# Attention decode over a long cache: scores and P·V on four 32-column TensorE tiles, with K^T and V as the moving operand

## Chip, cores, metric

One NeuronCore of one Trainium2 chip. The metric is the device time of one execution in microseconds, where smaller is better. Kernels are compared only within the same rounds. "Span" is the time from the first to the last instruction in a profile; in these runs the device time is about 1.8 us more than the span.

## The reference

A decode step for a single token (batch 1, query length 1, width 512). Attention has 32 query heads and 8 key/value heads of 128, over a cache of 32768 positions. Beside it runs a small gated feed-forward part, and a scalar gate mixes the two. All inputs are bfloat16. Cut to what matters:

```python
q = (x @ wq)                                   # 32 heads of 128
scores = einsum("bhqd,bhkd->bhqk", q, k) * Dh ** -0.5
p = softmax(scores)                            # over 32768 positions
a = einsum("bhqk,bhkd->bhqd", p, v) @ wo       # wo: 4096 x 512
b = (silu(x @ w_gate) * (x @ w_up)) @ w_down
g = sigmoid((x * gate_w).sum())
return g * a + (1 - g) * b
```

The K and V caches are 8 heads x 32768 x 128 x 2 bytes x 2 = 134 MB. With the weights, 148.1 MB have to be read, each byte once, with little arithmetic per byte.

## The kernel before

The loads form one stream into a ring of five slots of 4 MB. The stream's unit is a *half*: one half of the positions of one K or V head, 16384 x 128. Order: Wq, K halves of head 0 with the feed-forward weights between, then K of head g alternating with V of head g-1, then the last head's two V halves, and Wo at the very end. A slot is loaded again as soon as its former content is used.

```python
stream = [("wq",), ("K", 0, 0), ("F1",), ("K", 0, 1), ("F2",)]
for g in range(1, G):
    for hf in range(2):
        stream += [("K", g, hf), ("V", g - 1, hf)]
stream += [("V", G - 1, 0), ("V", G - 1, 1), ("wo",)]
...
# sync engine: one load per entry, once the slot's former content is released
if i >= NSLOT:
    sp.wait_ge(*released[stream[i - NSLOT]])
```

TensorE transposes K, 64 transposes per half. VectorE copies each group of four out of PSUM, the memory in which TensorE's results lie (`ktT`). The scores take K^T as the *stationary* operand: 128 weight loads per half, each followed by a matmul of only 8 columns. P·V, the exponentials times V, takes the exponentials as stationary operand (16 columns) and V as moving operand (512 columns): 32 matmuls per half, one after another.

```python
def emit_scores(j):
    ...
    for t in range(0, TPF, 2):
        for e in range(2):
            pe.matmul(ps_sc[f % NSC][:, col : col + 2 * HPG],
                      kt[:, e, :],            # stationary: K^T, 128 columns
                      qz[:, g, e, :],         # moving: q, 8 columns
                      start=(e == 0), stop=(e == 1))

def emit_pv(g, hf, src, r0, n):
    ...
    for r in range(r0, r0 + n, TPV):
        pe.matmul(ps_pv[0 : TPV * HPG, :],                       # 16 x 512
                  ET[:, g % NEG, k : k + TPV, :]...,             # stationary: 16 columns
                  src[:, r : r + TPV, :]...,                     # moving: V, 512 columns
                  start=(k == 0), stop=(k == NT - TPV))
    ...
def emit_o(g):      # fold the block diagonal of ps_pv (copied to pv_sb) into the head outputs
    ...
# (cut) after the last P·V: normalise, reorder heads, 128 Wo matmuls of one column, output
```

Of the kernel before, what the change touches and what calls it, by code (L numbers as in the profile page):

```python
# [13 lines left out]
def bass_gated_mix__gqa_block_cached__swiglu_ffn__decode_kernel(  # L14
# [18 lines left out]
    HPG = H // G  # L33
# [19 lines left out]
    TPV = 4  # L53
    NKT = 8
    NST = 3
    NSC = 3
    NEG = 3
    LAG = 3
    SCALE = float(DH) ** -0.5
    V_LAST = (64, 32, 16, 16)  # L60
    WO_CUT = (16, 8, 4, 4)
    assert sum(V_LAST) == RH and sum(WO_CUT) == WOJ
# [9 lines left out]
    with ExitStack() as es:  # L72
# [7 lines left out]
        sem_ld = [S_(f"s_ld{i}") for i in range(len(stream) - 2)]  # L80
        sem_ldv = [S_(f"s_ldv{i}") for i in range(len(V_LAST))]
# [38 lines left out]
        sem_osel = S_("s_osel")  # L120
        sem_pvc = S_("s_pvc")
# [13 lines left out]
        ET = T("ET", [128, NEG, NT, HPG], BF16)  # L135
# [22 lines left out]
        qz = T("qz", [128, G, 2, 2 * HPG], BF16)  # L158
# [3 lines left out]
        pmaxf = T("pmaxf", [128, NH, HPG], FP32)  # L162
        pmax = T("pmax", [128, G, HPG], FP32)
        gmax = T("gmax", [128, G, HPG], FP32)
        nbias = T("nbias", [128, G, HPG], FP32)
        esum = T("esum", [128, G, 2, HPG], FP32)
        esum2 = T("esum2", [128, G, HPG], FP32)
        rS = T("rS", [128, H], FP32)
        oidx = T("oidx", [128, TPV * HPG], FP32)
        osel = T("osel", [128, TPV, HPG], FP32)  # L170
        pv_sb = T("pv_sb", [TPV * HPG, TPV * DH], FP32)
# [11 lines left out]
        ps_sc = [ps[:, NST + i, :] for i in range(NSC)]  # L183
        ps_pv = ps[:, 6, :]
# [35 lines left out]
        with nc.Block("main") as block:  # L220

            @block.gpsimd
            def _(pool):
                npool = [0]

                def chain(ins):
# [42 lines left out]
                    oidx[:, :],  # L269
                    pattern=[[HPG, TPV], [1, HPG]],  # L270
                    base=0,
                    channel_multiplier=0,
                    allow_small_or_imprecise_dtypes=True,
                ).then_inc(sem_iota, 1)
                pool.iota(
# [6 lines left out]
                for g in range(G):  # L282
                    pool.wait_ge(sem_pmax, 3 * (g + 1))
                    pool.partition_all_reduce(  # L284
                        gmax[:, g, :], pmax[:, g, :], 128, ReduceOp.max
                    ).then_inc(sem_gmax, 1)

            @block.sync
            def _(sp):
                for i, e in enumerate(stream):  # L290
# [25 lines left out]
                    else:  # L316
# [5 lines left out]
                        if e == ("V", G - 1, 1):  # L322
                            r0 = 0
                            for c, n in enumerate(V_LAST):
                                sp.dma_start(
                                    dst[:, r0 : r0 + n, :], src[:, r0 : r0 + n, :]
                                ).then_inc(sem_ldv[c], 16)
                                r0 += n
                        else:
                            sp.dma_start(dst, src).then_inc(sem_ld[i], 16)  # L330
# [7 lines left out]
            def _(pe):  # L338
# [84 lines left out]
                def emit_scores(j):  # L423
                    f, q = j // FPH, j % FPH
                    g = f // 2
                    if j == 0:
                        pe.wait_ge(sem_qz, 4)
                    if q == 0 and f >= NSC:
                        pe.wait_ge(sem_exp, HPG * (f - NSC + 1))
                    pe.wait_ge(sem_cp, j + 1)  # L430
                    for t in range(0, TPF, 2):
                        col = (q * TPF + t) * HPG
                        kt = ktT[:, j % NKT, t * 128 : (t + 2) * 128].rearrange(
                            "p (k e) -> p e k", e=2
                        )
                        for e in range(2):
                            ins = pe.matmul(  # L437
                                ps_sc[f % NSC][:, col : col + 2 * HPG],
                                kt[:, e, :],
                                qz[:, g, e, :],  # L440
                                start=(e == 0),
                                stop=(e == 1),
                            )
                    ins.then_inc(sem_sc, 1)

                def emit_pv(g, hf, src, r0, n):
                    if r0 == 0 and hf == 0 and g > 0:
                        pe.wait_ge(sem_pvc, g)
                    for r in range(r0, r0 + n, TPV):
                        k = hf * RH + r  # L450
                        ins = pe.matmul(  # L451
                            ps_pv[0 : TPV * HPG, :],
                            ET[:, g % NEG, k : k + TPV, :].rearrange("p r h -> p (r h)"),
                            src[:, r : r + TPV, :].rearrange("p r d -> p (r d)"),
                            start=(k == 0),
                            stop=(k == NT - TPV),
                        )
                    if r0 + n == RH:
                        ins.then_inc(sem_pv, 1)

                def emit_o(g):
# [3 lines left out]
                    for r in range(TPV):  # L465
                        ins = pe.matmul(  # L466
                            ps_m[:, M_OT + g * HPG : M_OT + (g + 1) * HPG],
                            pv_sb[:, r * DH : (r + 1) * DH],
                            osel[0 : TPV * HPG, r, :],
                            start=(r == 0),  # L470
                            stop=(r == TPV - 1),
                        )
# [7 lines left out]
                for e in stream[:-1]:  # L480
                    if e[0] == "K":
                        pe.wait_ge(load_sem(e), 16)
                        for q in range(FPH):
                            emit_fill(filled, kv_slot(e), q)
                            filled += 1
                            if q >= LAG:
                                emit_scores(scored)
                                scored += 1
                            if e[2] == 0 and e[1] >= 2 and q == LAG:
                                emit_o(e[1] - 2)  # L490
                        continue
                    if e[0] != "V":
                        while scored < filled:
                            emit_scores(scored)
                            scored += 1
# [3 lines left out]
                    src = kv_slot(e)  # L499
                    pe.wait_ge(sem_exp, 2 * HPG * g + HPG * (hf + 1))  # L500
                    if e == ("V", G - 1, 1):
                        pe.wait_ge(sem_esum2, 1)
# [3 lines left out]
                            esum2[:, :, :].rearrange("p g h -> p (g h)"),  # L506
# [3 lines left out]
                        emit_o(G - 2)  # L510
                        r0 = 0
                        for c, n in enumerate(V_LAST):
                            pe.wait_ge(sem_ldv[c], 16)
                            emit_pv(g, hf, src, r0, n)
                            r0 += n
                        continue
                    pe.wait_ge(load_sem(e), 16)
                    r0 = 0
                    while scored < filled:
                        emit_pv(g, hf, src, r0, TPF)  # L520
                        r0 += TPF
                        emit_scores(scored)
                        scored += 1
                    emit_pv(g, hf, src, r0, RH - r0)
# [28 lines left out]
            def _(act):  # L553
# [10 lines left out]
                for g in range(G):  # L564
                    act.wait_ge(sem_gmax, g + 1)
                    act.activation(  # L566
                        nbias[:, g, :], gmax[:, g, :], ACT.Copy, scale=-SCALE
                    ).then_inc(sem_nbias, 1)
                    act.wait_ge(sem_nbias, g + 1)
                    if g >= NEG:  # L570
                        act.wait_ge(sem_pv, 2 * (g - NEG + 1))
                    for hf in range(2):
                        f = 2 * g + hf
                        sc = ps_sc[f % NSC].rearrange("p (t h) -> p h t", h=HPG)
                        for h in range(HPG):
                            act.activation(  # L576
                                ET[:, g % NEG, hf * RH : (hf + 1) * RH, h],
                                sc[:, h, :],
                                ACT.Exp,
                                bias=nbias[:, g, h : h + 1],  # L580
                                scale=SCALE,
                                accum_out=esum[:, g, hf, h : h + 1],
                            ).then_inc(sem_exp, 1)

            @block.vector
            def _(dve):
# [6 lines left out]

                dve.wait_ge(sem_pe_x, 1)
# [10 lines left out]
                dve.wait_ge(sem_iota, 4)  # L605
                for i, thr in enumerate((32.0, 64.0, 96.0)):
# [14 lines left out]
                dve.tensor_copy(pmat[:, :], pmat_f[:, :]).then_inc(sem_pm, 1)  # L621
                dve.tensor_scalar(
                    osel[:, :, :].rearrange("p r h -> p (r h)"),
                    oidx[:, :],
                    kf[:, 0:1],
                    None,
                    op0=ALU.is_equal,
                ).then_inc(sem_osel, 1)
# [9 lines left out]
                for e in range(2):  # L638
# [3 lines left out]
                    for b in range(2):  # L642
                        dve.tensor_copy(
                            qz[b * 64 : (b + 1) * 64, :, e, b * HPG : (b + 1) * HPG],
# [24 lines left out]
                def emit_pmax(f):  # L669
                    dve.wait_ge(sem_sc, FPH * (f + 1))  # L670
                    sc = ps_sc[f % NSC].rearrange("p (t h) -> p h t", h=HPG)
                    dve.tensor_reduce(pmaxf[:, f, :], sc, AX.X, ALU.max).then_inc(sem_pmax, 1)  # L672
                    if f % 2 == 1:
                        g = f // 2
                        dve.wait_ge(sem_pmax, 3 * g + 2)
# [82 lines left out]
```

## Time and profile before

| | before |
|---|---|
| median of 3 runs | 359.77 us (359.49 to 359.95) |
| profiled span, mean granted TensorE clock | 357.9 us, 0.967 |
| loads | 148.1 MB; 4 MB alone take 9.8 us at 429 GB/s |
| TensorE busy | 92% |

First the head of the profile's page: busy time of each engine, share of the span, instructions.

```profile
span 357.9 us, 9051 instructions
## 1 busy us (share of the span) xinstructions
PE 327.6 (92%) x4088; PEld 244.8 (68%) x4088; DVE 191.1 (53%) x321; ACT 28.5 (8%) x140; POOL 5.1 (1%) x23
```

TensorE looks like the bound. The next view, busy time of every engine in one stretch of the middle (columns: stretch, its length, busy times, granted TensorE clock, share of the 16 DMA engines, GB/s), says that it is not alone:

```profile
core 0: us, PE busy (x) PEld busy (x) DVE busy (x) ACT busy (x) POOL busy (x), PEclk, DMA share, GB/s
100.00:300.00 200.00, 194.66 (x2321) 142.23 (x2321) 116.76 (x184) 16.00 (x85) 1.86 (x5) 0.99 1.00 429
```

TensorE is busy 194.7 of 200 us, but the DMA engines are busy all of it, at 429 GB/s. The two are level.

The costliest TensorE groups (busy us, mean ns of one | idle before it, and what ended that): transposes of K, P·V, scores.

```profile
L418 PE MATMUL ps<-ident_f,ring 128*128 128x128 f32 x1024 | 161.8, 290 | 9.8 <-DMA ring<-in_A_k_cache_dram 9.8
L451 PE MATMUL ps<-ring,ET 128*16 128x512 bf16 x512 | 120.2, 379 | 0.9 <-DVE pv_sb L684 0.9
...
L437 PE MATMUL ps<-qz,ktT 128*128 128x8 bf16 x2048 | 88.4, 167 | 0.4 <-DVE ktT L690 0.4
```

The two groups that the change is about take 120.2 and 88.4 us. What TensorE waited for, in the list of waits (us in total, times, longest):

```profile
PE ps L418 <- DMA ring<-in_A_k_cache_dram: 9.8, 8, 6.0
```

Only 9.8 us in the whole execution. The end of the span, TensorE alone, in order of time:

```profile
333.45 7.07 PE L451 MATMUL ps<-ring,ET 128*16 128x512 bf16 x32 [0.86 <-DVE pv_sb L684]
...
341.77 7.07 PE L451 MATMUL ps<-ring,ET 128*16 128x512 bf16 x32
349.67 1.05 PE L466 MATMUL ps<-osel,pv_sb 16*128 16x4 f32 x8 [0.82 <-DVE pv_sb L684]
...
351.72 3.57 PE L538 MATMUL ps<-O,ring 128*128 128x1 bf16 x128 [0.28 <-DVE O L716]
```

The last two V halves follow each other without a gap of the load's making, 7.07 us each; then the fold, the Wo matmuls, and the output. The same stretch by what the loads did (columns as above):

```profile
342.00:344.00 2.00, 2.00 (x11) 0.87 (x10) 0.00 (x0) 0.00 (x0) 0.00 (x0) 1.00 1.03 432
...
346.00:348.00 2.00, 2.00 (x11) 0.81 (x9) 0.00 (x0) 0.00 (x0) 0.00 (x0) 1.00 0.64 268
...
350.00:352.00 2.00, 1.18 (x18) 1.00 (x18) 0.60 (x3) 0.00 (x0) 0.00 (x0) 0.86 0.50 203
352.00:354.00 2.00, 2.00 (x81) 2.00 (x79) 0.00 (x0) 0.00 (x0) 0.00 (x0) 0.50 0.02 8
```

The loads fade from 346 us on and are over soon after 352, yet TensorE's last Wo matmul ends at 351.72 + 3.57 = 355.29. At the end TensorE is late.

### The profile page before, as it was taken

Reading aid. Unit: us, or ns where it says so; the run is one execution under the profiler, and the core shown is the slowest. Engines: PE = TensorE matmul, PEld = TensorE weight load, DVE = VectorE, ACT = ScalarE, POOL = GpSimd, SP = SyncE. Lnnn points to the kernel's source line nnn. Section 1 sums busy time; section 2 is a strip of 40 time slices with the busy share of each in tenths; the row PEclk is TensorE's granted clock in tenths of the full one; section 3 lists DMA queues with packets and bytes.
Section 4 is the critical chain, followed back from the end, with each engine's and each line's share of the span. In section 5 each row is a group of like instructions: output and inputs, shape, how many; then the busy total and the mean of one; then the engine's idle time right before and its main releaser. Section 6 shows DMA issues by size and latency. Waiting matters only on the chain.

```text
span 357.9 us, 9051 instructions
## 1 busy us (share of the span) xinstructions
PE 327.6 (92%) x4088; PEld 244.8 (68%) x4088; DVE 191.1 (53%) x321; ACT 28.5 (8%) x140; POOL 5.1 (1%) x23
## 2 busy tenths in 40 slices
PE   0439999999999998999999999999999999999995
PEld 0439999858594957777584939686685949585345
DVE  0229197839292936657391918465472919384001
ACT  1000005000300030000300030001100030003000
POOL 0100000000000000000000000000000000000000
PEclk9999588999999999999999999999989999999996
DMA  8999999999999999999999999999999999999981
GB/s 344 417 405 452 416 431 430 434 419 430 441 416 437 430 430 430 423 436 425 426 435 423 438 423 428 438 430 419 439 420 427 441 416 443 427 423 421 412 365 75
DMA packets 6242, 148.69 MB, mean 415 GB/s; under 512 B 698, under 2 KB 700, under 8 KB 1212
## 3 DMA queue, kind: packets, MB, share of 16 engines
q1 hardware_dynamic: 6200, 148.12, 96.9%
q8 instruction: 32, 0.52, 0.6%
q14 instruction: 6, 0.05, 0.0%
q10 hardware_dynamic: 4, 0.00, 0.0%
HBM read 148.11 MB, written 0.00 MB: 414 GB/s over the span
## 4 chain that ended last, share of the span: by engine, by line
PE 56%; DMA 40%; DVE 2%; issue 1%; SPq 0%; DVEq 0%
DMA ring<-in_A_k_cache_dram 40%; PE ps L418 23%; PE ps L451 20%; PE ps L437 8%; PE ps L387 2%; PE ps L466 1%; PE ps L538 1%; DVE pv_sb L684 1%; DVE ktT L690 1%; PE ps L401 0%; SPq L294 0%; PE ps L503 0%; PE ps L548 0%; DVE row L729 0%; DVE res L720 0%
## 5 line engine op out<-in xcount | busy, mean ns | idle before, releaser
L690 DVE COPY ktT<-ps 128x1024 bf16<-128x1024 bf16 x256 | 168.5, 688 | 96.3 <-PE ps L418 96.0
L418 PE MATMUL ps<-ident_f,ring 128*128 128x128 f32 x1024 | 161.8, 290 | 9.8 <-DMA ring<-in_A_k_cache_dram 9.8
L418 PEld LDWEIGHTS ps<-ident_f,ring 128*128 128x128 f32 x1024 | 113.6, 145 | 18.0 <-DMA ring<-in_A_k_cache_dram 14.7
L451 PE MATMUL ps<-ring,ET 128*16 128x512 bf16 x512 | 120.2, 379 | 0.9 <-DVE pv_sb L684 0.9
L437 PEld LDWEIGHTS ps<-qz,ktT 128*128 128x128 bf16 x2048 | 85.6, 97 | 21.3 <-issue 18.1
L437 PE MATMUL ps<-qz,ktT 128*128 128x8 bf16 x2048 | 88.4, 167 | 0.4 <-DVE ktT L690 0.4
L451 PEld LDWEIGHTS ps<-ring,ET 128*16 128x16 bf16 x512 | 41.3, 89 | 52.4 <-issue 1.3
L672 DVE TENSOR_REDUCE pmaxf<-ps 128x4 f32<-128x512 f32 x16 | 11.1, 692 | 28.1 <-PE ps L437 28.1
L576 ACT ACTIVATE ET<-ps,nbias 128x128 bf16<-128x128 f32 x64 | 23.9, 556 | 0.2
L566 ACT ACTIVATE nbias<-gmax 128x4 f32<-128x4 f32 x8 | 1.6, 205 | 260.8 <-POOL gmax L284 260.8
L576 ACT ACTIVATION_READ_ACCUMULATOR ET<-ps,nbias 128x1 f32 x64 | 18.2, 284 | 0.0
L684 DVE COPY pv_sb<-ps 16x512 f32<-16x512 f32 x8 | 5.4, 671 | 12.5 <-PE ps L451 12.5
L466 PE MATMUL ps<-osel,pv_sb 16*128 16x4 f32 x64 | 8.4, 250 | 3.0 <-DVE pv_sb L684 3.0
L466 PEld LDWEIGHTS ps<-osel,pv_sb 16*128 16x128 f32 x64 | 7.7, 186 | 4.0 <-DVE pv_sb L684 3.5
L345 PE MATMUL ps<-ones_bf,x_row 1*128 1x1 bf16 x4 | 0.3, 172 | 7.8 <-DMA gw_row<-in_gate_w_dram 7.8
L284 POOL PARTITION_ALL_REDUCE gmax<-pmax x8 | 3.0, 374 | 311.9 <-DVE pmax L676 311.9
L362 PE MATMUL ps<-xT,ring 128*128 128x1 bf16 x128 | 3.6, 165 | 3.7 <-DMA ring<-in_A_wq_dram 3.7
L387 PE MATMUL ps<-xT,ring 128*128 128x1 bf16 x112 | 6.9, 198 | 0.0
L387 PEld LDWEIGHTS ps<-xT,ring 128*128 128x128 bf16 x112 | 6.8, 163 | 0.0
L362 PEld LDWEIGHTS ps<-xT,ring 128*128 128x128 bf16 x128 | 3.5, 104 | 3.7 <-issue 3.7
L345 PEld LDWEIGHTS ps<-ones_bf,x_row 1*128 1x128 bf16 x4 | 0.2, 115 | 7.8 <-DMA gw_row<-in_gate_w_dram 7.8
L595 DVE CAST xT<-ps 128x4 bf16<-128x4 f32 x1 | 0.2, 163 | 8.2 <-PE ps L345 8.2
(62 smaller groups left out, 26.4 us busy)
## 6 DMA issues: line engine op xcount, KB each, us to landing
ring<-in_A_k_cache_dram SPq DMA_DIRECT2D x16, 4096.0 KB, 39.5
ring<-in_A_v_cache_dram SPq DMA_DIRECT2D x15, 4096.0 KB, 38.0
ring<-in_A_wq_dram SPq DMA_DIRECT2D x1, 4096.0 KB, 12.3
ring<-in_A_v_cache_dram SPq DMA_DIRECT2D x1, 2048.0 KB, 32.2
ring<-in_A_wo_dram SPq DMA_DIRECT2D x1, 2048.0 KB, 33.8
ring<-in_B_w_gate_dram SPq DMA_DIRECT2D x1, 1792.0 KB, 26.5
ring<-in_B_w_up_dram SPq DMA_DIRECT2D x1, 1792.0 KB, 30.3
ring<-in_B_w_down_dram SPq DMA_DIRECT2D x1, 1792.0 KB, 43.4
```

The source lines that it names most:

```text
L284: pool.partition_all_reduce(gmax[:, g, :], pmax[:, g, :], 128, ReduceOp.max).then_inc(sem_gmax, 1)
L362: ins = pe.matmul(ps_m[:, M_Q0 + h : M_Q0 + h + 1], wq_v[:, c, h * DH : (h + 1) * DH], xT[:, c : c + 1], start=(c == 0), stop=(c == KC - 1),)
L387: ins = pe.matmul(ps_m[:, base + j : base + j + 1], wt[:, c, :].rearrange("d (p j) -> d j p", j=FC)[:, j, :], xT[:, c : c + 1], start=(c = ...
L418: ins = pe.transpose(stb[:, t * 64 : (t + 2) * 64], two.bitcast(FP32), ident_f[:, :])
L437: ins = pe.matmul(ps_sc[f % NSC][:, col : col + 2 * HPG], kt[:, e, :], qz[:, g, e, :], start=(e == 0), stop=(e == 1),)
L451: ins = pe.matmul(ps_pv[0 : TPV * HPG, :], ET[:, g % NEG, k : k + TPV, :].rearrange("p r h -> p (r h)"), src[:, r : r + TPV, :].rearrange( ...
L466: ins = pe.matmul(ps_m[:, M_OT + g * HPG : M_OT + (g + 1) * HPG], pv_sb[:, r * DH : (r + 1) * DH], osel[0 : TPV * HPG, r, :], start=(r == ...
L538: ins = pe.matmul(ps_a[:, oc, :], wo_v[:, j, oc * 128 : (oc + 1) * 128], O2[:, j : j + 1], start=(j == 0), stop=(j == WOJ - 1),)
L576: act.activation(ET[:, g % NEG, hf * RH : (hf + 1) * RH, h], sc[:, h, :], ACT.Exp, bias=nbias[:, g, h : h + 1], scale=SCALE, accum_out=esu ...
L672: dve.tensor_reduce(pmaxf[:, f, :], sc, AX.X, ALU.max).then_inc(sem_pmax, 1)
L684: dve.tensor_copy(pv_sb[:, :], ps_pv[0 : TPV * HPG, :]).then_inc(sem_pvc, 1)
L690: dve.tensor_copy(ktT[:, j % NKT, :], pst[j % NST]).then_inc(sem_cp, 1)
```

## The change

The intent is to give TensorE less to do. Scores and P·V use the array as four tiles of 32 columns that work at the same time; the long operand streams through as the moving one. A half's scores become 32 matmuls of 512 columns; P·V keeps its 32 matmuls, four at a time, to four quarters of PSUM's partitions. Since scores now lie as (head and position block) x positions, one exp per half suffices, but P has to be transposed back by TensorE (4 transposes) and copied. The last V half is loaded in one piece instead of four. The diff cut to its core:

```diff
-                    for t in range(0, TPF, 2):
-                        ...
-                        for e in range(2):
+                    for e in range(2):
+                        for c in range(NCG):
+                            kt = ktT[:, (NCG * b + c) % NKT, :].rearrange("p (k e) -> p e k", e=2)
                             ins = pe.matmul(
-                                ps_sc[f % NSC][:, col : col + 2 * HPG],
-                                kt[:, e, :],
-                                qz[:, g, e, :],
+                                ps_sc[f % NSC][32 * c : 32 * c + 32, :],
+                                qz[:, g, e, 24 - PB * i : 56 - PB * i],
+                                kt[:, e, :],
...
+                def emit_pt(f):              # transpose P back, four 128 x 128
...
-                            ps_pv[0 : TPV * HPG, :],
+                                    ps_pv[32 * c : 32 * c + 2 * PB, :],
...
-                        if e == ("V", G - 1, 1):
-                            for c, n in enumerate(V_LAST): ...   # four loads
-                        else:
-                            sp.dma_start(dst, src).then_inc(sem_ld[i], 16)
+                        sp.dma_start(dst, src).then_inc(sem_ld[i], 16)
...
-                        for h in range(HPG):                     # scalar engine: four exps
+                    act.activation(P[:, f % 2, :], ps_sc[f % NSC], ACT.Exp, ...)   # one
```

(cut: the masks that let one exp serve four heads, the fold over four quarters, buffers)

## The prediction

> **What bounds the kernel now.** The DMA stream. In the 20 us windows from 20 to 320 us the DMA engines are busy 0.98 to 1.02 of the time and move 419 to 437 GB/s; the page gives 148.1 MB read. The Trainium skill, "DMA: Bandwidth & Descriptors", section "Where 436 GB/s comes from", puts the ceiling at 435 GB/s; this trace agrees. TensorE is a close second (PE 92%): one K half plus one V half takes it 18.5 to 21 us (from the load issues), just what 8.4 MB take at 430 GB/s. But about four transfers stay queued (a K load lands 38.5 us after issue; alone it needs 9.8), so DMA never starves.
>
> The 1 us windows show the end: DMA keeps 385 to 446 GB/s until 346 us, then about 230 GB/s (some engines finish earlier) until 351.7. The last V half lands near 341.3 us (issue plus time to landing). TensorE is late there too: the timeline has the last two V halves back to back, 333.45 to 340.5 and 341.77 to 348.84 us, then pv_sb and its fold until 350.7, 128 Wo matmuls 351.72 to 355.29; the span ends at 357.9.
>
> **What the change does.** Per half, scores go from 128 weight loads and 128 matmuls of 8 columns (0.34 us per 8, 5.5 us) to 32 matmuls of 512 columns on four column tiles; P·V stays at 32 such matmuls, now four at a time, instead of 7.05 us. At 0.22 us per matmul full overlap gives 1.8 us each. The skill, "TensorE: Matmul & The Clock Gate", section "Measured speedup vs the span model", gives 2.38x for three column tiles; I take about 3x for four, 2.4 us each (estimate; no trace shows it yet). Added: 4 transposes of P (0.4 us) and a 128x512 copy (under 0.7 us, the cost of pv_sb's). Four exps of 0.55 us become one of about 0.7. Unchanged: 64 transposes of K, 8 to 10 us, and 16 copies of 688 ns. TensorE falls to about 14 us per pair, partly paced by VectorE's 11 us of copies.
>
> **On the critical path.** In the middle nothing: slots come free sooner, but DMA is saturated. Only the tail gains. The last P·V starts at its landing (341.4), takes 2.4 to 4.5 us (after idling, the clock may be at half), copy 0.7, fold 1.1 to 1.5, about 1 us to O2: 347 to 349.5. Then Wo waits for its own load, whose last piece lands at about 351.7; 16 matmuls (0.5 us) and the same 2.6 us of end follow: span about 355. Time is 1.9 us more: 357.0.
>
> **Prediction: 357.0 us, 8 in 10 within 354.8 to 360.3.** Faster by over 2%: 0.03. Within 2%: 0.91. Slower by over 2%: 0.06.
>
> **What would show it.** DMA stays at 425 to 437 GB/s and ends at 351 to 352 us. PE share falls to 60 to 75%; scores and P·V occupy at most half their former time (the tiles may be recorded overlapping). TensorE waits 4 to 7 us per pair for loads. The granted clock falls below 0.97. In the tail the last P·V starts on its load, and the final Wo matmuls wait for Wo's load.
>
> **What would make it wrong.** Column tiles that run one after another (TensorE about 23 us per pair, some 400 us); half clock throughout; drains between 128-wide and 32-wide modes; four moving streams slowing DMA writes or VectorE. On the other side, a DMA end that comes earlier because slots come free sooner: then 2% is within reach.

## The result

| | before | after |
|---|---|---|
| median | 359.84 us (4 runs) | 357.35 us (4 runs, 356.87 to 357.70) |
| ratio | | 0.9931, 95% interval 0.9914 to 0.9949 |
| profiled span, granted clock | 357.9 us, 0.967 | 355.8 us, 0.851 |
| TensorE busy | 92% | 72% |

A ratio here is the mean time of one kernel's fast runs over that of the other's of the same rounds, so not quite the ratio of the medians. The result is 0.7% faster: within 2%.

The page's head after, then the same 200 us of the middle:

```profile
span 355.8 us, 6082 instructions
...
PE 257.5 (72%) x2616; PEld 191.4 (54%) x2616; DVE 198.2 (56%) x372; ACT 14.5 (4%) x36; POOL 5.6 (2%) x22
```

```profile
100.00:300.00 200.00, 149.72 (x1385) 110.12 (x1385) 119.81 (x208) 7.23 (x20) 1.85 (x5) 0.86 1.00 430
```

TensorE's busy time fell from 194.7 to 149.7 us of 200; the loads moved 430 instead of 429 GB/s. The granted clock in that stretch fell from 0.99 to 0.86. TensorE's groups in the same order (transposes, scores, P·V):

```profile
L415 PE MATMUL ps<-ident_f,ring 128*128 128x128 f32 x1024 | 164.3, 321 | 57.0 <-DMA ring<-in_A_k_cache_dram 57.0
...
L431 PE MATMUL ps<-ktT,qz 128*32 128x512 bf16 x512 | 41.8, 403 | 15.2 <-DVE ktT L726 15.1
L463 PE MATMUL ps<-ring,ET 128*16 128x512 bf16 x512 | 33.4, 406 | 5.4 <-DMA ring<-in_A_v_cache_dram 5.4
```

Scores went from 88.4 to 41.8 us, P·V from 120.2 to 33.4; the transposes stayed. The mean of one matmul (about 400 ns) did not fall, because four overlap: busy time per group is what to read here. The list of waits shows where the time went:

```profile
PE ps L415 <- DMA ring<-in_A_k_cache_dram: 57.0, 14, 5.8
...
PE ps L463 <- DMA ring<-in_A_v_cache_dram: 5.4, 1, 5.4
```

9.8 us of waiting for K became 57.0, and there is a wait of 5.4 us for the last V half. The time saved on TensorE in the middle turned into waiting. The end, TensorE alone:

```profile
333.17 3.59 PE L463 MATMUL ps<-ring,ET 128*16 128x512 bf16 x32
...
342.74 3.21 PE L463 MATMUL ps<-ring,ET 128*16 128x512 bf16 x32 [5.41 <-DMA ring<-in_A_v_cache_dram]
346.81 1.05 PE L479 MATMUL ps<-osel,pv_sb 128*128 128x4 f32 x8 [0.86 <-DVE pv_sb L719]
...
348.87 3.15 PE L542 MATMUL ps<-O,ring 128*128 128x1 bf16 x112 [0.29 <-DVE O L765]
352.57 0.58 PE L542 MATMUL ps<-O,ring 128*128 128x1 bf16 x16 [0.56 <-DMA ring<-in_A_wo_dram]
```

The last P·V starts when its load has landed, at 342.7. The last 16 Wo matmuls wait 0.56 us for Wo's last piece. The loads at the end, to be held against those of before:

```profile
342.00:344.00 2.00, 1.26 (x16) 0.42 (x20) 0.00 (x0) 0.00 (x0) 0.00 (x0) 0.50 0.92 385
...
346.00:348.00 2.00, 1.05 (x8) 0.97 (x8) 0.79 (x2) 0.00 (x0) 0.00 (x0) 1.00 0.59 242
...
350.00:352.00 2.00, 2.00 (x76) 1.93 (x73) 0.00 (x0) 0.00 (x0) 0.00 (x0) 0.50 0.12 47
352.00:354.00 2.00, 0.87 (x18) 0.58 (x17) 0.33 (x2) 0.00 (x0) 0.00 (x0) 0.50 0.00 0
```

The chain of waits that ended last says the same. Its last long link is Wo's load (start, length, what):

```profile
310.63 41.89 DMA ring<-in_A_wo_dram
...
352.57 0.60 PE ps L542 x16
```

So the loads end in both kernels near 352.5 to 353 us, and TensorE's last Wo matmul ended at 355.29 before and ends at 353.15 after. That is the 2.1 us of the span.

One more look at the middle: how fast TensorE runs depends on how long it idled before.

```profile
273.79 3.29 PE L415 MATMUL ps<-ident_f,ring 128*128 128x128 f32 x24 [1.25 <-DMA ring<-in_A_k_cache_dram]
277.11 0.64 PE L431 MATMUL ps<-ktT,qz 128*32 128x512 bf16 x8
277.68 1.53 PE L415 MATMUL ps<-ident_f,ring 128*128 128x128 f32 x12
...
293.21 4.53 PE L415 MATMUL ps<-ident_f,ring 128*128 128x128 f32 x20 [5.80 <-DMA ring<-in_A_k_cache_dram]
```

After an idle of 1.25 us, 24 transposes take 3.29 us (scores on tiles follow). After 5.80 us, 20 of them take 4.53. In this trace the granted clock fell to 0.50 at 290.8 us, within the longer idle, and was 1.00 again from 297.6. So part of the saving is given back, at no cost while the loads are the bound.

### The profile page after: what moved, and what is told of

Read it like the earlier page. It is cut to its first block, busy times and chain, and to the rows that moved or that the text cites. A ratio compares the mean times of both kernels' runs of the same rounds, so it can differ in the third digit from the quotient of the medians.

```text
span 355.8 us, 6082 instructions
## 1 busy us (share of the span) xinstructions
PE 257.5 (72%) x2616; PEld 191.4 (54%) x2616; DVE 198.2 (56%) x372; ACT 14.5 (4%) x36; POOL 5.6 (2%) x22
## 4 chain that ended last, share of the span: by engine, by line
DMA 67%; PE 29%; DVE 2%; issue 1%; SPq 0%; DVEq 0%
DMA ring<-in_A_k_cache_dram 55%; PE ps L415 18%; DMA ring<-in_A_wo_dram 12%; PE ps L431 5%; PE ps L463 2%; PE ps L384 2%; DVE ktT L726 1%; PE ps L479 0%; PE ps L398 0%; SPq L317 0%; PE ps L445 0%; PE ps L542 0%; SPq L299 0%; PE ps L552 0%; DVE row L778 0%
## 5 line engine op out<-in xcount | busy, mean ns | idle before, releaser
L415 PEld LDWEIGHTS ps<-ident_f,ring 128*128 128x128 f32 x1024 | 141.0, 167 | 89.5 <-DMA ring<-in_A_k_cache_dram 63.6
L431 PE MATMUL ps<-ktT,qz 128*32 128x512 bf16 x512 | 41.8, 403 | 15.2 <-DVE ktT L726 15.1
L463 PE MATMUL ps<-ring,ET 128*16 128x512 bf16 x512 | 33.4, 406 | 5.4 <-DMA ring<-in_A_v_cache_dram 5.4
L463 PEld LDWEIGHTS ps<-ring,ET 128*16 128x16 bf16 x512 | 13.1, 94 | 22.2 <-DMA ring<-in_A_v_cache_dram 5.5
L431 PEld LDWEIGHTS ps<-ktT,qz 128*32 128x32 bf16 x512 | 7.9, 95 | 28.0 <-DVE ktT L726 24.4
L573 ACT ACTIVATE P<-ps,nbias 128x512 bf16<-128x512 f32 x16 | 10.8, 682 | 273.6 <-DVE nbias L703 273.6
L682 DVE TENSOR_REDUCE pmaxf<-ps 128x1 f32<-128x512 f32 x16 | 11.1, 692 | 11.9 <-PE ps L431 11.9
L479 PEld LDWEIGHTS ps<-osel,pv_sb 128*128 128x128 f32 x64 | 10.0, 237 | 1.7 <-DVE pv_sb L719 1.7
L479 PE MATMUL ps<-osel,pv_sb 128*128 128x4 f32 x64 | 9.6, 274 | 1.0 <-DVE pv_sb L719 0.9
L711 DVE COPY ET<-ps 128x512 bf16<-128x512 bf16 x16 | 6.7, 416 | 1.3 <-PE ps L445 1.3
```

What stands on the lines that cost most here:

```text
L415: ins = pe.transpose(stb[:, t * 64 : (t + 2) * 64], two.bitcast(FP32), ident_f[:, :])
L431: ins = pe.matmul(ps_sc[f % NSC][32 * c : 32 * c + 32, :], qz[:, g, e, 24 - PB * i : 56 - PB * i], kt[:, e, :], start=(i == 0 and e == 0), ...
L463: ins = pe.matmul(ps_pv[32 * c : 32 * c + 2 * PB, :], ET[:, f % NET, col : col + 2 * PB], src.rearrange("p (i c t) d -> p i c t d", i=NI, ...
L479: ins = pe.matmul(ps_m[:, M_OT + g * HPG : M_OT + (g + 1) * HPG], pv_sb[:, r * DH : (r + 1) * DH], osel[:, r * HPG : (r + 1) * HPG], start ...
L573: act.activation(P[:, f % 2, :], ps_sc[f % NSC], ACT.Exp, bias=nbias[:, f // 2 : f // 2 + 1], scale=SCALE, accum_out=esum[:, f // 2, f % 2 ...
L682: ins = dve.tensor_reduce(pmaxf[:, f : f + 1], ps_sc[f % NSC], AX.X, ALU.max)
```

## The experiments

Theory A: in the middle the loads set the pace, so no TensorE time there is worth anything; the gain is the tail alone, where P·V no longer makes TensorE late. Rival B: the gain comes from loads that end earlier, since fewer TensorE instructions have to be fetched by the DMA engines. (The page counts 32 instruction packets of 16 KB on one queue before and 20 after.) Rival C: TensorE time in the middle counts. Theory D and rival E came up on the way.

| run | kernel | median us | ratio to before, 95% interval |
|---|---|---|---|
| e1_pv_tiles | before + P·V on tiles | 357.88 | 0.9931 (0.9899 to 0.9964) |
| e2_pv_one_tile | after, P·V undone | 361.18 | 1.0018 (0.9986 to 1.0050) |
| e3_pv_twice | after, P·V twice in the middle | 357.07 | 0.9914 (0.9884 to 0.9945) |
| e4_light | after, a quarter of TensorE's work | 357.51 | 0.9918 (0.9890 to 0.9945) |
| e6_wo_eight | after, last MB of Wo on 8 engines | 363.00 | 1.0084 (1.0060 to 1.0108) |
| e7_warm | after, 12 spare matmuls | 357.51 | 0.9935 (0.9918 to 0.9952) |
| e8_balance | after, V and Wo pieces on 8 engines | 369.51 | 1.0277 (1.0261 to 1.0292) |
| e9_balance_warm | e8 and e7 | 369.74 | 1.0275 (1.0260 to 1.0290) |
| e13_after_again | after | 357.22 | 0.9929 (0.9913 to 0.9945) |
| e10_wo_short | after, 1 MB less of Wo | 356.63 | 0.9916 (0.9897 to 0.9936) |
| e12_warm_longer | after, 24 spare matmuls | 357.27 | 0.9926 (0.9913 to 0.9938) |
| e11_wo_short_warm | e10 and e12 | 355.67 | 0.9882 (0.9867 to 0.9897) |

The first four ran in one set of rounds, the next four in another, the last four in a third. A median is to be held only against others of its own set.

### One part alone: P·V on tiles

```diff
 # in the kernel before
-                            ps_pv[0 : TPV * HPG, :],
+                            ps_pv[32 * c : 32 * c + TPV * HPG, :],      # c = (k // TPV) % 4
```

(and the fold over four quarters, taken from the kernel after)

> The kernel before with one part of the change: P·V on four column tiles, scores and exps as before. Theory A (the middle is set by the loads; the gain is TensorE's late tail, two V halves of 7 us back to back): nearly the whole gain, 357.6 us (356.8 to 358.5); last P·V starts on its load near 342 us, Wo waits for its own last piece near 352.5. Rival B (the gain comes from loads that end earlier, because fewer TensorE instructions have to be fetched by the same DMA engines, 20 fetches of 16 KB after against 32 before): 32 fetches stay, so no gain, 359.5. Rival C (TensorE time saved in the middle counts): part of the gain, about 358.2, and the score share of it missing.

Measured: 357.88 us, ratio 0.9931, the same ratio as the whole change. Two lines of TensorE's tail, the last half but one and the last Wo matmuls:

```profile
333.17 3.59 PE L453 MATMUL ps<-ring,ET 128*16 128x512 bf16 x32 [5.41 <-DMA ring<-in_A_v_cache_dram]
...
352.86 0.59 PE L540 MATMUL ps<-O,ring 128*128 128x1 bf16 x16 [0.65 <-DMA ring<-in_A_wo_dram]
```

P·V on tiles alone brings the gain; the new scores, the single exp and the transposes of P add nothing to it that can be seen. This kernel has 32 instruction fetches like the kernel before, so rival B's 359.5 is out. Rival C's 358.2 is too near to be told by this run. One thing speaks against a part of the change: here the last V half still comes in four loads, and its P·V is over at 343.61 us (last four matmuls 343.01 + 0.60), against 345.95 in the kernel after, which loads it in one piece. The kernel after with four loads was not run.

### The other part alone: P·V undone

```diff
 # in the kernel after
-                                    ps_pv[32 * c : 32 * c + 2 * PB, :],
+                                    ps_pv[0 : 2 * PB, :],
```

> The kernel after with P·V undone: the same 32 matmuls per half, all on column tile 0, so one after another. Theory A: a K half takes TensorE 13.5 us (paced by VectorE's copies) and P·V now 7 us, 20.5 us per pair against 19.4 us of loads, so TensorE becomes the bound and the tail is longer as well: 365 us (360 to 371). If only loads counted in the middle and TensorE never: about 362 (the tail alone, P·V of the last half 8 us on a clock that starts at half). Rival B (fetches alone): 357.4.

Measured: 361.18 us. The whole gain is gone. But theory A's number was too high: TensorE did not become the bound in the middle.

```profile
100.00:300.00 200.00, 186.23 (x1408) 112.12 (x1408) 119.18 (x213) 7.23 (x20) 1.85 (x5) 1.00 1.00 430
```

TensorE is busy 186.2 of 200 us at a granted clock of 1.00, and the loads still run at 430 GB/s. I had added 7 us to 13.5 us for a K half, and the 13.5 was measured after an idle, on a low clock; in this run a K half takes 11.7 us (273.41 to 285.12 us on TensorE's timeline), so a pair takes 18.8 us, under the 19.5 us of its loads at 430 GB/s. What is left is the tail, as in the second figure (362):

```profile
334.36 8.76 PE L463 MATMUL ps<-ring,ET 128*16 128x512 bf16 x32
...
343.39 7.07 PE L463 MATMUL ps<-ring,ET 128*16 128x512 bf16 x32
...
353.37 3.42 PE L542 MATMUL ps<-O,ring 128*128 128x1 bf16 x128 [0.29 <-DVE O L765]
```

The last two P·V again take 8.76 and 7.07 us back to back, and the Wo matmuls start at 353.37 instead of 348.87. The loads ended no later for it: the last V half landed at 342.3 and Wo's last piece at 352.1 (342.7 and 352.5 in the kernel after), so the loss is all in the tail.

### P·V in the middle doubled, and TensorE's work quartered

```diff
 # e3, in the kernel after (the sums are scaled to match)
+                            for rep in range(2 if g < G - 1 else 1):
                               for c in range(NCG): ...
 # e4, in the kernel after
-                    for t in range(0, TPF, 2):
+                    for t in range(0, TPF if j < NST else 2, 2):     # K transposes
-                        for c in range(NCG):
+                        for c in range(NCG if f < NSC else 1):       # scores
-                            for c in range(NCG):
+                            for c in range(NCG if g == 0 else 1):    # P·V
```

> The kernel after with every P·V matmul issued twice for groups 0 to 6 (the sums are corrected, the result stays right); the last group, and so the tail, is unchanged. Theory A: 1.9 us more TensorE per half fits into its wait for loads (about 6 us per pair): 357.4 us, no change. With theory B added: 3 to 4 more fetches, up to 0.6 us later: 358. Rival C (TensorE time in the middle counts): 14 halves x 1.9 us = 27 us more, 384.

Measured: 357.07 us.

```profile
100.00:300.00 200.00, 167.14 (x1710) 115.70 (x1710) 119.08 (x209) 7.23 (x20) 1.85 (x5) 0.89 1.00 430
```

> Wrong result on purpose: the kernel after with a quarter of the K transposes, scores and P·V matmuls, all loads, copies, exps and semaphores kept; about 3200 instructions instead of 6082, so about 9 instruction fetches instead of 20. Theory A alone (last Wo piece lands at 352.5 whatever TensorE does): 357.2. Theory B (each fetch takes a DMA engine about 1.5 us from the loads, 9 engines share them): the slowest engine ends 1.5 to 2.5 us earlier, 355.2 (354.3 to 356.2). Rival C: over 10 us faster.

Measured: 357.51 us. (Its result is wrong in what it computes, on purpose; the comparison with the reference still passed, so it says nothing of this kernel's arithmetic.)

```profile
100.00:300.00 200.00, 136.38 (x413) 56.28 (x412) 117.48 (x209) 7.23 (x20) 1.85 (x5) 0.62 1.00 432
```

TensorE's busy time in the 200 us is 167.1 with P·V doubled and 149.7 without, and the time is the same. With 3220 instructions instead of 6082 it is the same again; its busy time is still 136.4 us, at a granted clock of 0.62. Rival C is out.

The light run also settles B as it was put (fetches of TensorE's instructions): 9 instruction fetches instead of 20, and no gain. The trace shows why. A load on all 16 DMA engines lands in 16 parts; for Wo's last piece these are the times (us from the span's start), in order:

| | instruction fetches | first | 9th | 15th | last |
|---|---|---|---|---|---|
| before | 32 | 346.2 | 352.0 | 352.7 | 352.9 |
| after | 20 | 345.9 | 349.1 | 350.9 | 352.5 |
| e4_light | 9 | 346.2 | 347.7 | 347.9 | 352.4 |

Fewer fetches do bring most parts forward: the 9th by 4.3 us from before to e4_light. But one part is over 6 us behind the first in all three kernels, and the load is complete only with that one. So half of B was right and it is worth nothing: these fetches delay the middle of the field, and the last one holds the end.

The trace also shows what goes with the delay of that last part. The page lists two queues of instruction fetches, and from the kernel after to e4_light only the first changed (these lines are e4_light's):

```profile
q8 instruction: 9, 0.15, 0.2%
q14 instruction: 5, 0.04, 0.0%
```

The table above counts q8. The second, q14, has five 8 KB packets after the start in the kernel after and in e4_light alike, and six in the kernel before. In e4_light the last part's distance from the first grew by 0.65, 0.97, 0.95, 1.03 and 0.94 us in five of the loads that land after 50 us, and by at most 0.05 us in any other; in each of these five, one q14 packet ran (at 50.7, 107.5, 172.8, 243.0 and 305.9 us). In the kernel after it is the same: five steps, 4.7 of its 6.6 us. Such a packet took 0.32 us and the 32 KB packet that followed it 1.87 us instead of 1.22, about 1.0 us in all; a q8 fetch cost about 1.6 us in the same way. So it looks as if all q14 fetches fall on one DMA engine, which the load then waits for (the trace names no engines). The other 2 us or so were there by 47 us. No run took the q14 packets away, so this is read from the traces and not tested.

### Loads moved to eight engines

Theory D, formed before the q14 packets were noticed: take bytes from the slow engine. By the Trainium skill, "DMA: Bandwidth & Descriptors", section "Why a DMA increments its semaphore by 16 and not by 1", a transfer of 8 partitions runs on the 8 lowest-numbered engines. The trace of e6 agrees on the number: its 16 small transfers made 144 updates of their semaphore, one each at the issue and 128, 8 each, at landings. Which engines they were, no run here shows.

```diff
 # e6, in the kernel after
-    WO_CUT = (16, 8, 4, 4)
+    WO_CUT = (16, 8, 8)
+                            pp = 8 if c == len(WO_CUT) - 1 else 128
+                            for p0 in range(0, 128, pp):
+                                sp.dma_start(wo_v[p0 : p0 + pp, j0 : j0 + n, :], ...)
 # e8: the same for the last 32 of 128 rows of the last V half and the last 4 of 32 columns of Wo
 # e9: e8 with the 12 spare matmuls of e7
```

> The kernel after with the last 1 MB of Wo loaded by 16 transfers of 8 partitions each, which use 8 of the 16 DMA engines, instead of transfers of 128 partitions, which use all 16. Theory D (formed after the light kernel: one DMA engine falls 6.3 us behind whatever TensorE does, some seven never do, and the last load waits for the slow one): if the eight engines used are not the slow ones, the slow end comes 2.4 us earlier, about 350.1, and the end is then held by the chain from the last V half: 356.8 us. If the slow ones are among the eight: the loads end 2.4 us later, 359.7. No theory expects no change of the landings.

> The kernel after with 1 MB of the last V half and the last 0.5 MB of Wo in transfers of 8 partitions on 8 engines. Theory D with slow engines outside the eight: last V half lands 2.4 us earlier (about 340.3 on the slow engines), Wo near 349 to 350, time 354.8 us. With slow engines inside: about 361.

> The two runs before this one together (8-partition transfers and spare matmuls). Theory D with slow engines outside the eight: 354.4 us, up to 1.3 less than without the spare matmuls if the chain from the last V half holds the end, nothing if Wo's last piece does. With slow engines inside: 361.

Measured: 363.00, 369.51 and 369.74 us, all slower.

```profile
342.71 3.38 PE L466 MATMUL ps<-ring,ET 128*16 128x512 bf16 x32 [5.41 <-DMA ring<-in_A_v_cache_dram]
...
358.27 1.01 PE L545 MATMUL ps<-O,ring 128*128 128x1 bf16 x32 [3.90 <-DMA ring<-in_A_wo_dram]
```

In e6 the last V half started as ever (342.71), and the last Wo matmuls waited until 358.27. The gain of the first branch, slow engines outside the eight, did not come. But the second does not fit either: 2.4 us later was expected and it came 5.7 us later, and e8 lost over 12 us instead of 4. In the trace of e8 the 16 KB packets took 975 ns (median, after 300 us), against 614 in the kernel after. So the small transfers slowed others as well, and by what I can't say. What is shown: the kernel after, whose loads are spread over all 16 engines, is faster than these three. Whether the slow engine can be relieved stays open.

### The low clock in the tail

At the end of the kernel after, the last P·V takes 3.21 us and not the 1.90 of the middle, on a granted clock of 0.50 until 345.4 us. The Trainium skill, "TensorE: Matmul & The Clock Gate", section "Part 1: The HAM clock gate (the "warmup" mystery)", says that the clock is halved after an idle of about 3.4 us. In the middle this trace agrees: TensorE idled from 287.4 us and the clock fell at 290.8. In the tail an idle of that length does not explain it: the clock fell at 331.8 us, after idles of 1.20 and 0.61 us with four transposes after each, and was still low through the idle of 5.41 us before the last P·V. Rival E: this costs the change part of its gain.

```diff
 # e7 (12) and e12 (24), in the kernel after
+                    if e == ("V", G - 1, 1):
+                        for _ in range(12):
+                            pe.matmul(pst_f[1], ident[:, :], P[:, 0, :], start=True, stop=True)
                     pe.wait_ge(load_sem(e), 16)
```

> The kernel after with 12 spare matmuls of 512 columns while TensorE waits for the last V half, so that the clock is high: the last P·V takes 1.9 us instead of 3.2 to 3.6. Theory A (Wo's last piece holds the end, TensorE is 0.5 us early): 357.1 us, at most 0.3 faster. Rival E (the halved clock in the tail is what the change lost): 1.3 to 2 us faster, 355.7.

Measured: 357.51 us, but the edit had not done what it should. The spare matmuls were over 3.1 us before the load had landed, and the last P·V still took 2.87 us:

```profile
336.92 2.54 PE L529 MATMUL ps<-P,ident 128*128 128x512 bf16 x11
342.60 2.87 PE L463 MATMUL ps<-ring,ET 128*16 128x512 bf16 x32 [3.14 <-DMA ring<-in_A_v_cache_dram]
```

(The clock had risen to 1.00 at 336.6 and fell again at 343.4, in the midst of the P·V.) So this run is inconclusive, and the second has 24 of them.

### Two holders of the end, taken away one by one

```diff
 # e10, in the kernel after: no load for the last 8 of 32 columns of Wo (wrong result on purpose)
+                            if c >= 2:
+                                continue
                             sp.dma_start(wo_v[:, j0 : j0 + n, :], ...)
 # e12: 24 spare matmuls; e11: both; e13: the kernel after itself
```

> The kernel after, unchanged, in the same rounds as the next three, so that differences of half a microsecond can be read: 357.3 us (356.9 to 357.7).

> Wrong result on purpose: the kernel after without the last 1 MB of Wo (the matmuls stay and read what lies there). Theory A (two holders almost level: Wo's last piece near 352.5 and the chain from the last V half, whose Wo matmuls can end at 352.6): 0.5 us faster than the kernel after, 356.8, because the chain takes over. Rival (Wo's load alone holds the end): 2.4 us faster, 354.9.

> The kernel after with 24 spare matmuls before the last P·V (12 ended 3 us too early and the clock had fallen again: P·V took 2.87 us). Theory A: last P·V in about 1.9 us, but the end is still Wo's last piece: 357.2 us, within 0.3 of the kernel after. Rival E (the low clock of the tail costs time): 1.5 us faster, 355.8.

> Wrong result on purpose: the last two together, Wo short by 1 MB and 24 spare matmuls. Theory A: only now both holders are gone, about 2 us faster than the kernel after, 355.3 us, more than the sum of the two alone.

Measured: 357.22 (the kernel after), 356.63, 357.27, 355.67 us: alone 0.6 us and nothing, together 1.55 us. Single runs of the kernel after lie between 356.76 and 358.11, of e10 between 356.15 and 357.81, of e11 between 355.59 and 355.78. The intervals of e10 and of the kernel after overlap, so the 0.6 alone is not sure; that of e11 lies below it. TensorE's tail of the three, the last P·V and the last Wo matmuls. First Wo short:

```profile
342.04 3.59 PE L465 MATMUL ps<-ring,ET 128*16 128x512 bf16 x32 [5.84 <-DMA ring<-in_A_v_cache_dram]
...
348.55 3.52 PE L545 MATMUL ps<-O,ring 128*128 128x1 bf16 x128 [0.29 <-DVE O L768]
```

Nothing waits for Wo any more; its 128 matmuls follow the chain from the last V half. Then the spare matmuls:

```profile
342.56 1.90 PE L463 MATMUL ps<-ring,ET 128*16 128x512 bf16 x32
...
352.34 0.59 PE L547 MATMUL ps<-O,ring 128*128 128x1 bf16 x16 [0.65 <-DMA ring<-in_A_wo_dram]
```

P·V takes 1.90 us, 1.3 to 1.7 less, and all of it turns into waiting for Wo's last piece. Then both:

```profile
342.07 1.90 PE L465 MATMUL ps<-ring,ET 128*16 128x512 bf16 x32
...
349.39 1.87 PE L550 MATMUL ps<-O,ring 128*128 128x1 bf16 x64 [0.53 <-DMA ring<-in_A_wo_dram]
```

The last Wo matmuls are now over at 351.3, against 353.15 in the kernel after. (In the profiled execution of the kernel after in these rounds, e13, the chain was the later one: P·V took 3.59 us and the 128 Wo matmuls ran from 349.91 to 353.48 without waiting; so too in e3 and e7.) So at the end there are two chains almost level, the last V half with what follows it, and Wo's own load; only together do they give way. Rival E is out for the kernel as it is. Two microseconds expected, 1.55 measured: Wo's shorter load then holds the end itself.

No version with a right result beats the kernel after by more than the noise. The slack that is left belongs to the loads.

## Why the prediction was right

- *The loads are the bound.* Right: 429 GB/s before and 430 after, over 200 us of the middle; the time does not move when P·V there is doubled or TensorE's work is cut (e3, e4).
- *The cost of tiles.* I took three times for four tiles. The measured P·V went from 7.07 to 1.90 us per half, 3.7 times; eight score matmuls take 0.64 us as recorded. TensorE's time per pair came out as 149.7 / 200 x 19.5 = 14.6 us; 14 was predicted. That four tiles work nearly free of each other is what e1 rests on.
- *The middle gives nothing, the tail gives all.* Right, shown from both sides: P·V on tiles alone gives ratio 0.9931 (e1), the rest without it 1.0018 (e2).
- *The tail's terms.* The last V half was put at 341.3 to 341.4 us; it lands at 342.7 (and at 343.0 before). I had taken one issue time for four issues shown as one row. Wo's last piece was put at 351.7 and lands at 352.5: I read the end of the loads from the fall of the GB/s, and one engine trickles on behind that. P·V 3.21 us (2.4 to 4.5), copy 0.69, fold 1.05 (1.1 to 1.5), O2 at 348.8 (347 to 349.5): inside or just beside. The span, put at about 355, is 355.8, and the time 357.35 instead of 357.0. The terms that were off are the two landings, by 1.3 and 0.8 us. One term was left out, and here luck helped: the first 112 Wo matmuls need no last piece and take 3.15 us after O2. With O2 at the late end of the stated range, 349.5, they would have ended near 352.7, after the predicted landing of 351.7. In the profiled execution they ended at 352.0, 0.5 us before the landing of 352.5; in that of e13 this chain was the later one, and Wo's load held nothing. That there are two chains almost level was not in the prediction.
- *What would show it.* TensorE at 72% (60 to 75), clock 0.851 (below 0.97), scores at 47% and P·V at 28% of their former busy time (half at most), last P·V on its load, last Wo matmuls on theirs: all as said in the profiled execution, the last of them not in e13's. The wait for K loads, 57.0 us in 14 waits, is one of 5.1 us at the start and 13 in the pairs from 76 us on, 4.0 us each in the mean; 4 to 7 was predicted.
- *What would have made it wrong* did not come: no tiles in single file, no loads slowed by four moving streams. The low clock came; in the middle nobody waits for it, and in the tail it makes the chain from the last V half about as long as Wo's load (e10 to e12). On the other side, slots that come free sooner made the loads end hardly sooner (352.9 to 352.5).

## What to carry to other kernels

When two resources are level, find in the middle which one would stay if the other were free; if it is the loads, a faster engine buys idle time and a lower clock. Then look at the end by itself: after the loads only the work that hangs on the last piece counts, and what is late there, here P·V, is all that a change of the engine's speed can gain. Read the end of the loads from their last landing, not from the mean rate, and test a tail that has two chains by taking both away together.

## What the Trainium skill lacked or had wrong

- "TensorE: Matmul & The Clock Gate", section "Measured speedup vs the span model", has three column tiles (2.38x) and none with four. Here 32 matmuls of 16 x 512 outputs took 1.90 us on four column tiles against 7.07 in single file, 3.7x, at granted clock 1.00.
- "TensorEngine Tiling (Array Packing)", section "Key Properties", says that a change of tiling mode drains TensorE, without a figure. Here eight score matmuls on tiles between 128-wide transposes take 0.57 us from their first start to that of the next transpose (277.11 to 277.68 us); two rounds at 1.90 / 8 = 0.24 us each, an estimate, leave about 0.1 us for both changes.
- "Runtime: NRT & Kernel Launch", section "Instruction fetch mechanics", calls a fetch mostly hidden. For the engine that may be so; but in the kernels before and after each fetch of 16 KB took 0.9 to 1.1 us on the DMA engines that carry the loads, the 32 KB packet behind it took about 1.7 us instead of 1.22, and the 9th of 16 parts of the last load landed at 347.7, 349.1 and 352.0 us with 9, 20 and 32 fetches.
- "DMA: Bandwidth & Descriptors" gives no figure for how far the 16 engines drift apart over a long stream. Here the last part of the last load came 6.2 to 6.6 us after the first in the kernels before, after and light, whatever TensorE did; in after and light 4.7 and 4.5 us of it came in five steps, each in a load during which a q14 fetch of 8 KB ran.
- The same page tells which engines a transfer of 8 partitions uses, not what such transfers cost their neighbours: 16 KB packets took 975 ns in e8, with them, and 614 in the kernel after, without.
